# Attention's values move into the ring of five weight buffers, are asked for two groups ahead, and q and k get a sixth buffer

## The chip, the core and the metric

The kernel runs on one core of a Trainium2 chip. The core has five engines that run their own instruction streams in order and meet at semaphores: TensorE (PE, matrix products; its weight loads are shown as PEld), VectorE (DVE), ScalarE (ACT), GpSimd (POOL) and SyncE (SP, which here does nothing but issue transfers). Transfers between HBM and on-chip memory run on 16 DMA engines. The metric is device time in microseconds (us) of one execution, the median of the runs.

## What is computed

Three steps in a row: attention with a sigmoid instead of a softmax, a mixture of 8 experts in which every token gets exactly one expert, and a two-layer network with a squared ReLU.

```python
batch, n_heads, seq, head_dim = (4, 12, 448, 64)
scores = scale * np.matmul(q, k.transpose(0, 1, 3, 2)) - np.log(S)
attn = 1.0 / (1.0 + np.exp(-scores))
x = np.matmul(attn, v)                      # then laid out as 1792 tokens x 768
logits = x @ w_gate                         # 1792 x 8; greedy assignment, 224 tokens per expert
h = np.maximum(x[mask] @ w1[e], 0.0); out[mask] = h @ w2[e]
r = np.maximum(x @ w_in, 0.0); y = (s * (r * r) + b) @ w_out
```

The change lies in the first step alone.

## The kernel before

**Groups.** The 12 heads of 4 batches make 24 pairs of heads, and two pairs make a group: 12 groups (`NQ`), three to a batch. The loop `for q in range(NQ)` runs over the groups, and each pass has two halves.

**What one group costs each engine.** `scores(q + 1, ...)` makes the products of keys and queries of the next group on PE, in seven units of 128 (or, for unit 3, 2 x 64) keys; after each, ACT takes the sigmoid into a tile `attn`. Outside the first group a score is the sum of three products of rounded halves, `wh` and `wl`, which DVE makes from the raw q and k of a pair in `split_qk(n)` (two instructions). The small unit 3 takes the raw tile itself. `values(q, half)` then multiplies `attn` by the values: 12 PE instructions on blocks of 128 keys (line 334 in the first kernel) and, at the start of the second half, 8 on the last 64 keys of the two pairs (line 328). So 448 keys of two pairs are 2 x 3 blocks of 128 and one block that holds 64 of each pair.

**Other work in the loop.** DVE also converts the last network's weights in 24 pieces of 128 x 768 (`convert`, lines 152 to 169), each read as 768 KB (`cv_in`, tile `craw`, three buffers) and written back as 384 KB (`cv_out`, `nw<-co`). At the first group of batches 1 to 3 the gate of the batch before is worked out (`gate`, `gate_turn`, `prefs`), and in the last three groups four tiles of the first expert's weights are fetched and split (`w_dma` line 235, `w_high` line 244 on ACT, `w_low` line 254 on DVE).

**Order of the transfers.** Almost every transfer is issued by SP, in the order of the code, and SP stands still at each until what it overwrites is free: `cv_in` waits until DVE has read the `craw` tile (line 155), `cv_out` until the converted piece is done. Besides, each transfer waits until the one eight places before it has landed, since eight semaphores go round. In pass q SP is given q and k of pairs 2q + 5 and 2q + 6 (`load_qk`, lines 273 and 274, 224 KB each), then the values of group q + 1 (`load_v`, line 268, 448 KB), and behind them the pieces of the two conversions.

**Buffers.** Tile `rqk` holds q and k of one pair: five buffers. Tile `vt` holds the values of one group, 7 blocks of 128 x 128: two buffers. The ring `wraw`, five buffers of 6 blocks of 128 x 128 (384 KB), holds raw weights from the end of attention on and lies unused until then.

After the loop come the assignment of tokens to experts (the auction) and, with three quarters of the time, the experts and the last network, in which PE is fed from `wraw`.

Of the kernel before, what the change touches and what calls it, by code (L numbers as in the profile page):

```python
# [8 lines left out]
F32 = mybir.dt.float32  # L9
# [10 lines left out]
B, H, S, D = 4, 12, 448, 64  # L20
# [26 lines left out]
NQ = B * NP // 2  # L47
# [15 lines left out]


@with_exitstack
def tile_kernel(ctx, tc, qT, kT, v, wg, w1, w2, wi, wo, s2, b2, cst, out):
    nc = tc.nc
    V, A, G, T = nc.vector, nc.scalar, nc.gpsimd, nc.tensor

    const = ctx.enter_context(tc.tile_pool(name="const", bufs=1))  # L70
    wraw = ctx.enter_context(tc.tile_pool(name="wraw", bufs=5))
# [48 lines left out]
    cgp = early.enter_context(tc.tile_pool(name="cgp", bufs=1))  # L120

    att = ExitStack()
    qk = att.enter_context(tc.tile_pool(name="qk", bufs=5))
    vp = att.enter_context(tc.tile_pool(name="vp", bufs=2))
    at = att.enter_context(tc.tile_pool(name="at", bufs=2))
    ps_s = att.enter_context(tc.tile_pool(name="ps_s", bufs=3, space=PSUM))
# [9 lines left out]
    def cv_in():  # L136
        if todo:
            i = todo.pop(0)
            src, k, n = wide[i]
            craw[i] = cgp.tile([128, 768, 2], I32, name="craw", bufs=3)  # L140
            nc.sync.dma_start(craw[i].rearrange("p a b -> p (a b)"), src[n].bitcast(I32).rearrange("p k c -> p (k c)"))
            coming.append(i)
# [117 lines left out]
        nu["use"] += 1  # L260
        return splits.pop(i)

    raw_qk, two_qk, vt, attn, pvs, plg, lgs, pts = {}, {}, {}, {}, {}, {}, {}, {}
    pairs = [(b, p) for b in range(B) for p in range(NP)]

    def load_v(q):
        vt[q] = vp.tile([128, 7, 128], F32, name="vt", bufs=2)
        nc.sync.dma_start(vt[q], v[q // 3, q % 3])

    def load_qk(i):  # L270
        b, p = pairs[i]
        r = qk.tile([128, 2, S], F32, name="rqk")
        nc.sync.dma_start(r[:, 1], kT[b, p])
        nc.sync.dma_start(r[:, 0], qT[b, p])
        raw_qk[i] = r

    def split_qk(i):
        r = raw_qk[i]
        h = wsp.tile([128, 2 * S], F32R, name="wh")
        lo = wlp.tile([128, 2 * S], F32R, name="wl")  # L280
        r = r.rearrange("p a s -> p (a s)")
        V.tensor_copy(h, r)
        V.tensor_sub(lo, r, h.bitcast(F32))
        two_qk[i] = [a.rearrange("p (a s) -> p a s", a=2) for a in (h, lo)]
# [4 lines left out]
    def scores(q, units):  # L289
        if q >= NQ:  # L290
            return
        for r in units:
            p = ps_s.tile([128, 2, 512], F32, name="psc")
            if r == 3:
                work = [(2 * q + n, slice(HD, S), slice(n * 64, n * 64 + 64)) for n in range(2)]
            else:
                c = r % 4
                work = [(2 * q + r // 4, slice(c * 128, (c + 1) * 128), slice(0, 128))]
            plain = q < PLAIN or r == 3
            n_terms = 1 if plain else 3  # L300
            for m in range(n_terms):
                for j in range(2):
                    me = slice(j * D, (j + 1) * D)
                    for n, keys, rows in work:
                        if plain:
                            kx = qx = raw_qk[n]
                        else:
                            h, lo = two_qk[n]
                            kx, qx = ((h, h), (lo, h), (h, lo))[m]
                        T.matmul(p[rows, j, :S], kx[me, 1, keys], qx[me, 0], start=(m == 0),  # L310
                                 stop=(m == n_terms - 1), skip_group_check=True)
            attn[q, r] = at.tile([128, 2, S], F32, name="attn", bufs=8)
            A.activation(attn[q, r], p[:, :, :S], AF.Sigmoid, bias=nls, scale=1.0 / math.sqrt(D))  # L313
        if units[-1] == 6:
            for n in (2 * q, 2 * q + 1):
                raw_qk.pop(n)
                if q >= PLAIN:
                    two_qk.pop(n)

    def values(q, block):  # L320
        v = vt[q]
        pvs[q, block] = pv = ps_v.tile([128, 512], F32, name="pv")
        if block:
            a = attn.pop((q, 3))
            for n in range(2):
                rows = slice(n * 64, n * 64 + 64)
                for j in range(2):
                    T.matmul(pvs[q, n][j * 64:(j + 1) * 64, :S], v[rows, 3, j * D:(j + 1) * D], a[rows, j],
                             start=(n == 1), stop=(n == 0), skip_group_check=True)
            done(q, 0)  # L330
        for c in range(3):
            a = attn.pop((q, 4 * block + c))
            for j in range(2):
                T.matmul(pv[j * 64:(j + 1) * 64, :S], v[:, 4 * block + c, j * D:(j + 1) * D], a[:, j],  # L334
                         start=(block == 0 and c == 0), stop=(block == 1 and c == 2), skip_group_check=True)
        if block:
            done(q, 1)

    def done(q, n):
        b, p = pairs[2 * q + n]  # L340
        pv = pvs.pop((q, n))
        xt = xT[:, p, b * S:(b + 1) * S]
        if (q, n) == (NQ - 1, 1):
            A.copy(xt[:, :2 * CP], pv[:, :2 * CP])
            A.copy(xt[:, 2 * CP:], pv[:, 2 * CP:S])
        else:
            A.copy(xt, pv[:, :S])
# [9 lines left out]
    def gate_copy(b):  # L357
        lgs[b] = at.tile([128, S], F32, name="lg", bufs=1)
        A.copy(lgs[b], plg.pop(b)[:, :S])
# [65 lines left out]
    load_qk(1)  # L425
    nc.sync.dma_start(ct, cst)
    load_v(0)
    G.memset(wgs, 0.0)
    nc.sync.dma_start(wgs[:, :, :E], wg)
    load_qk(2)  # L430
    load_qk(3)
    cv_in()
    cv_in()
    cv_in()
    scores(0, range(7))
    load_qk(4)
    nc.sync.dma_start(sb2[:, 0:1], s2.partition_broadcast(128))
    nc.sync.dma_start(sb2[:, 1:2], b2.partition_broadcast(128))
    G.memset(on, 1.0)
# [12 lines left out]
    for q in range(NQ):  # L452
        b, t = divmod(q, 3)
        closing = b == B - 1
        for n in (2 * q + 5, 2 * q + 6):
            if n < 2 * NQ:
                load_qk(n)
        if q + 1 < NQ:
            load_v(q + 1)
        for half in range(2):  # L460
            if q + 2 < NQ:
                split_qk(2 * q + 4 + half)
            values(q, half)
            if t == 0 and b:
                if half:
                    gate_turn(b - 1, True)
                    prefs(b - 1)
                else:
                    gate(b - 1, 0, NP, NP)
                    gate_copy(b - 1)  # L470
            if closing and 1 <= 2 * t + half <= 4 and 2 * t + half != 2:
                bracket((2 * t + half) // 2)
            if closing and t == 2 and not half:
                gate(b, 0, NP - 2, NP - 2)
                gate_copy(b)
            scores(q + 1, range(4, 7) if half else range(4))
            n = 2 * (NQ - q) - half
            if 2 < n <= 6:
                w_dma()
            for _ in range({4: 1, 3: 1, 2: 2}.get(n, 0)):  # L480
                w_high()
            for _ in range(CONV[2 * q + half]):
                convert()
            while nu["low"] < nu["high"]:
                w_low()
# [800 lines left out]
def _layout(np, i):  # L1286
    c = np.ascontiguousarray

    def heads(a):
        return a.reshape(B, NP, 2, S, D)  # L1290

    vv = i["v"].reshape(B, 3, 2, 2, S, D)
    main = (vv[..., :HD, :].reshape(B, 3, 2, 2, 3, 128, D).transpose(0, 1, 2, 5, 4, 3, 6)
            .reshape(B, 3, 2, 128, 3, 128))
    tail = vv[..., HD:, :].transpose(0, 1, 2, 4, 3, 5).reshape(B, 3, 128, 1, 128)

    return {
        "qT": c(heads(i["q"]).transpose(0, 1, 2, 4, 3).reshape(B, NP, 128, S)),
        "kT": c(heads(i["k"]).transpose(0, 1, 2, 4, 3).reshape(B, NP, 128, S)),
        "v": c(np.concatenate([main[:, :, 0], tail, main[:, :, 1]], axis=3)),  # L1300
        "wg": c(i["moe_w_gate"].reshape(KD, 128, E).transpose(1, 0, 2)),
        "w1": c(i["moe_w1"].reshape(E, KD, 128, KF, 128).transpose(0, 3, 2, 1, 4)),
        "w2": c(i["moe_w2"].reshape(E, KF, 128, KD, 128).transpose(0, 3, 1, 2, 4).reshape(E, KF, KD, 128, 128)
                .transpose(0, 1, 3, 2, 4)),
        "wi": c(i["moe2_w_in"].reshape(KD, 128, KG, 128).transpose(2, 1, 0, 3)).view(np.int64),
        "wo": c(i["moe2_w_out"].reshape(8, 2, 128, 2, DH).transpose(3, 0, 2, 1, 4)
                .reshape(KG, 128, KD, 128)).view(np.int64),
        "s2": c(i["moe2_s"]),
        "b2": c(i["moe2_b"]),
        "cst": _consts(np),  # L1310
    }
# [17 lines left out]
```

## Time and profile before

| | before |
|---|---|
| median of 3 runs | 881.94 us (879.71 to 887.55) |
| profiled execution, time | 882.63 us |
| profiled execution, span of the core | 880.8 us |
| PE busy | 856.3 us, 97% of the span |
| PEld / DVE / ACT / POOL busy | 746.9 / 642.6 / 509.4 / 85.0 us |
| mean granted TensorE clock | 0.987 |
| attention | from the start to about 158 us |

Times in the trace are microseconds from the start of the span. Attention is the part in which PE's rows carry `psc` (scores, gate) and `pv` (values). In a timeline or chain row the first number is the start, the second the length; an "x12" merges twelve instructions of one line, and square brackets give the idle time ahead of the row and what ended it. The granted clock is given as a share of full speed: 1.00 is 2.4 GHz and 0.50 is 1.2 GHz.

### The profile page before, as it was taken

To read this page: it belongs to the slowest core of one execution; us is meant where nothing else is said; L and a number is where in the kernel's file an instruction comes from. 1 tells how busy PE (TensorE), PEld (TensorE's weight loads), DVE (VectorE), ACT (ScalarE), POOL (GpSimd) and SP (SyncE) were. 2 spreads that over 40 slices of the span, in tenths; PEclk is the share of its full clock that TensorE was granted. 3 is DMA by queue.
4 is the path that set the end of the run, shared out by engine and by line. 5 is a ranking of instruction groups with operands and counts; after the bars stand their busy time and mean duration, and the time that the engine had idled before them with its cause. 6 is when DMAs were issued, how large, how long until landed. Compare 5 with 4: busy or idle time off the path is not lost.

```text
span 880.8 us, 14238 instructions
## 1 busy us (share of the span) xinstructions
PE 856.3 (97%) x5188; PEld 746.9 (85%) x5188; DVE 642.6 (73%) x1113; ACT 509.4 (58%) x887; POOL 85.0 (10%) x146
## 2 busy tenths in 40 slices
PE   9898999879999999999999999999999999999997
PEld 4444454649999999999999999999999999999997
DVE  2978786756778776779768776877887766857681
ACT  6466567745755566753565546767666555645440
POOL 1000000123000000000155422000000000000003
PEclk9899999999999999999999999999999999999999
DMA  8889796666668786658899987676653433332313
GB/s 297 303 295 353 268 381 231 187 205 223 208 200 287 244 291 208 209 187 304 280 335 319 301 238 247 194 234 185 225 180 98 128 107 116 112 106 91 101 37 132
DMA packets 76778, 190.40 MB, mean 216 GB/s; under 512 B 9120, under 2 KB 31136, under 8 KB 76448
## 3 DMA queue, kind: packets, MB, share of 16 engines
q1 hardware_dynamic: 68800, 164.28, 55.7%
q0 software_dynamic: 7904, 25.17, 10.1%
q8 instruction: 42, 0.69, 0.3%
q14 instruction: 32, 0.26, 0.1%
HBM read 161.11 MB, written 42.47 MB: 231 GB/s over the span
## 4 chain that ended last, share of the span: by engine, by line
PE 89%; DMA 5%; DVE 2%; ACT 1%; issue 1%; SPq 1%; POOL 0%; POOLq 0%; DVEq 0%; ACTq 0%
PE acc L757 16%; PE acc L758 8%; PE acc L1072 7%; PE acc L1071 7%; PE acc L1069 7%; PE pv L334 6%; PE psc L310 5%; PE acc L915 4%; PE acc L914 4%; PE acc L916 4%; PE acc L1178 4%; PE acc L1180 4%; PE acc L1179 4%; DMA vt<-in_v_dram 3%; PE acc L783 1%; PE acc L784 1%
## 5 line engine op out<-in xcount | busy, mean ns | idle before, releaser
L244 ACT CAST wh<-raw 128x768 fp32r<-128x768 f32 (+1 forms) x248 | 201.5, 823 | 91.0 <-issue 66.5
L254 DVE TENSOR_TENSOR wl<-raw,wh 128x768 fp32r<-128x768 f32 (+1 forms) x248 | 229.5, 937 | 21.3 <-PE acc L1071 11.3
L757 PE MATMUL acc<-u,wh 128*128 128x448 f32 x384 | 120.8, 374 | 0.0
L758 PE MATMUL acc<-u,wl 128*128 128x224 f32 x384 | 101.6, 265 | 0.2 <-DVE wl L254 0.2
L757 PE MATMUL acc<-x,wh 128*128 128x448 f32 x288 | 95.0, 384 | 0.6 <-issue 0.6
L313 ACT ACTIVATE attn<-psc,nls 128x896 f32<-128x896 f32 x84 | 78.0, 1009 | 29.9 <-PE psc L310 29.9
L758 PE MATMUL acc<-x,wl 128*128 128x224 f32 x288 | 76.9, 267 | 0.0
L757 PEld LDWEIGHTS acc<-u,wh 128*128 128x128 f32 x384 | 72.0, 188 | 5.3
L758 PEld LDWEIGHTS acc<-u,wl 128*128 128x128 f32 x384 | 73.3, 191 | 0.4 <-DVE wl L254 0.4
L334 PE MATMUL pv<-attn,vt 128*64 128x448 f32 x288 | 62.9, 574 | 8.5 <-DMA vt<-in_v_dram 8.5
L914 PE MATMUL acc<-y,wh 128*128 128x448 f32 x192 | 70.8, 369 | 0.0
L915 PE MATMUL acc<-y,wh 128*128 128x448 f32 x192 | 70.2, 366 | 0.0
L916 PE MATMUL acc<-y,wl 128*128 128x448 f32 x192 | 70.1, 365 | 0.0
L762 ACT COPY tmp<-acc 128x224 f32<-128x224 f32 x96 | 33.0, 343 | 48.9 <-PE acc L758 48.6
L757 PEld LDWEIGHTS acc<-x,wh 128*128 128x128 f32 x288 | 55.0, 191 | 4.8 <-issue 0.9
L334 PEld LDWEIGHTS pv<-attn,vt 128*64 128x64 f32 x288 | 19.7, 141 | 44.5 <-issue 41.6
L1069 PE MATMUL acc<-wh,as 128*128 128x384 f32 x168 | 56.1, 334 | 0.0
L1071 PE MATMUL acc<-wl,as 128*128 128x384 f32 x168 | 56.1, 334 | 0.0
L1072 PE MATMUL acc<-wh,as 128*128 128x384 f32 x168 | 56.1, 334 | 0.0
L758 PEld LDWEIGHTS acc<-x,wl 128*128 128x128 f32 x288 | 55.8, 194 | 0.3 <-DVE wl L254 0.3
L763 DVE TENSOR_TENSOR tmp<-acc,tmp 128x224 f32<-128x224 f32 x78 | 30.1, 385 | 27.9 <-ACT tmp L762 27.5
L648 POOL DMA_INDIRECT xr<-xs,idx x16 | 16.8, 1050 | 262.2 <-PE px L748 250.1
(338 smaller groups left out, 1974.2 us busy)
## 6 DMA issues: line engine op xcount, KB each, us to landing
raw<-in_w_dram SPq DMA_DIRECT2D x128, 384.0 KB, 3.8
raw<-nw SPq DMA_DIRECT2D x64, 384.0 KB, 3.7
craw<-in_wi_dram SPq DMA_DIRECT2D x16, 768.0 KB, 6.6
raw<-mx SPq DMA_DIRECT2D x32, 384.0 KB, 5.0
nw<-co SPq DMA_DIRECT2D x24, 384.0 KB, 7.3
craw<-in_wo_dram SPq DMA_DIRECT2D x8, 768.0 KB, 6.1
ra<-in_wo_dram SPq DMA_DIRECT2D x8, 768.0 KB, 5.3
hs<-nw POOLq DMA_DIRECT2D x16, 384.0 KB, 9.7
```

Source lines behind the costliest of these rows:

```text
L244: A.copy(h, r)
L254: eng.tensor_sub(lo, r, h.bitcast(F32))
L313: A.activation(attn[q, r], p[:, :, :S], AF.Sigmoid, bias=nls, scale=1.0 / math.sqrt(D))
L334: T.matmul(pv[j * 64:(j + 1) * 64, :S], v[:, 4 * block + c, j * D:(j + 1) * D], a[:, j], start=(block == 0 and c == 0), stop=(block == 1 a ...
L757: T.matmul(p[:, :2 * CAP], wh, src[:, k].rearrange("p a s -> p (a s)"), start=(k == 0), stop=False)
L758: T.matmul(p[:, :CAP], wl, src[:, k, 0], start=False, stop=(k == n - 1))
L914: T.matmul(p, wh, src[:, k, 0], start=first, stop=False)
L915: T.matmul(p, wh, src[:, k, 1], start=False, stop=False)
L916: T.matmul(p, wl, src[:, k, 0], start=False, stop=last)
L1069: T.matmul(acc, hi, wh[:, cols], start=(opens[j] and u == 0 and c == 0), stop=False, skip_group_check=True)
L1071: T.matmul(acc, hi, wl[:, cols], start=False, stop=False, skip_group_check=True)
L1072: T.matmul(acc, lo, wh[:, cols], start=False, stop=(u == 3 and c == 1), skip_group_check=True)
```

## The change

Four things, all in attention:

1. The values of a group are a tile of the ring `wraw` (six blocks, 384 KB, name `raw`), and `vt`'s two buffers are gone.
2. The blocks that hold the last 64 keys are taken out of `v` into an input of their own, `vrest`: one tile `vr` of three blocks (192 KB, two buffers) for the three groups of a batch, loaded with the batch's first group.
3. `load_v` runs two groups ahead: in pass q it asks for group q + 2, and group 1 is asked for before the loop, between the first and the second `cv_in`.
4. `rqk` has six buffers, and `load_qk` runs one pair further ahead: pairs 4 and 5 are asked for before the first scores, and pass q asks for 2q + 6 and 2q + 7.

```diff
 def load_v(q):
-    vt[q] = vp.tile([128, 7, 128], F32, name="vt", bufs=2)
+    vt[q] = wraw.tile([128, 6, 128], F32, name="raw")
     nc.sync.dma_start(vt[q], v[q // 3, q % 3])
+    if q % 3 == 0:
+        vr[q // 3] = vp.tile([128, 3, 128], F32, name="vr")
+        nc.sync.dma_start(vr[q // 3], vrest[q // 3])

-    qk = att.enter_context(tc.tile_pool(name="qk", bufs=5))
+    qk = att.enter_context(tc.tile_pool(name="qk", bufs=6))

 def values(q, block):
-    v = vt[q]
+    v, rest = vt[q], vr[q // 3][:, q % 3]
...
-                T.matmul(..., v[rows, 3, j * D:(j + 1) * D], a[rows, j], ...)
+                T.matmul(..., rest[rows, j * D:(j + 1) * D], a[rows, j], ...)
...
-            T.matmul(..., v[:, 4 * block + c, j * D:(j + 1) * D], a[:, j], ...)
+            T.matmul(..., v[:, 3 * block + c, j * D:(j + 1) * D], a[:, j], ...)

 load_qk(2)
 load_qk(3)
 cv_in()
+load_v(1)
 cv_in()
 cv_in()
+load_qk(4)
+load_qk(5)
 scores(0, range(7))
-load_qk(4)

 for q in range(NQ):
-    for n in (2 * q + 5, 2 * q + 6):
+    for n in (2 * q + 6, 2 * q + 7):
         if n < 2 * NQ:
             load_qk(n)
-    if q + 1 < NQ:
-        load_v(q + 1)
+    if q + 2 < NQ:
+        load_v(q + 2)
```

The instructions of PE, DVE, ACT and POOL stay the same and in the same order; SP has four transfers more (the four `vr`) and another order. Line numbers behind line 268 grow by three to five: 310 becomes 313, 334 becomes 337.

The start of SP's queue before, from the first conversion tile on. `craw` is a conversion tile, `rqk` q or k of a pair (here pairs 4, 5 and 6), `sb` two constants, `vt` the values of group 1; in brackets what the transfer waits for (DMAHW is the transfer eight places before it):

```order
L141 DMA craw<-in_wi_dram 128x1536 [waits DMAHW3_49]
L141 DMA craw<-in_wi_dram 128x1536 [waits DMAHW4_49]
L141 DMA craw<-in_wi_dram 128x1536 [waits DMAHW5_49]
L273 DMA rqk<-in_kT_dram 128x448 [waits DMAHW6_49]
L274 DMA rqk<-in_qT_dram 128x448 [waits DMAHW7_49]
L437 DMA sb_76<-in_s_dram 128x1 [waits DMAHW0_49]
L438 DMA sb_76<-in_b_dram 128x1 [waits DMAHW1_49]
L273 DMA rqk<-in_kT_dram 128x448 [waits DMAHW2_49,PE_49]
L274 DMA rqk<-in_qT_dram 128x448 [waits DMAHW3_49]
L273 DMA rqk<-in_kT_dram 128x448 [waits DMAHW4_49,PE_49]
L274 DMA rqk<-in_qT_dram 128x448 [waits DMAHW5_49]
L268 DMA vt<-in_v_dram 128x896 [waits DMAHW6_49]
```

The same place of the changed kernel, up to the constants; the `raw` tile is the values of group 1, and the two pairs are 4 and 5:

```order
L141 DMA craw<-in_wi_dram 128x1536 [waits DMAHW4_49]
L268 DMA raw<-in_v_dram 128x768 [waits DMAHW5_49]
L141 DMA craw<-in_wi_dram 128x1536 [waits DMAHW6_49]
L141 DMA craw<-in_wi_dram 128x1536 [waits DMAHW7_49]
L276 DMA rqk<-in_kT_dram 128x448 [waits DMAHW0_49]
L277 DMA rqk<-in_qT_dram 128x448 [waits DMAHW1_49]
L276 DMA rqk<-in_kT_dram 128x448 [waits DMAHW2_49]
L277 DMA rqk<-in_qT_dram 128x448 [waits DMAHW3_49]
L442 DMA sb_76<-in_s_dram 128x1 [waits DMAHW4_49]
L443 DMA sb_76<-in_b_dram 128x1 [waits DMAHW5_49]
```

Group 1's values moved from behind pair 6 to ahead of the second conversion tile, and pairs 4 and 5 stand behind them, 384 KB later than before; ahead of this place one `vr` tile was added.

The other end of attention, SP's queue in passes 10 and 11 before: the last group's values, the third and fourth tile of expert weights and the last converted pieces:

```order
L268 DMA vt<-in_v_dram 128x896 [waits DMAHW5_49,PE_49]
L235 DMA raw<-in_w_dram 128x768 [waits DMAHW6_49]
L147 DMA nw_156<-co 128x768 [waits DMAHW7_49,DVE_49]
L235 DMA raw<-in_w_dram 128x768 [waits DMAHW0_49]
L147 DMA nw_157<-co 128x768 [waits DMAHW1_49,DVE_49]
```

And in the changed kernel, where the last values were already asked for in pass 9:

```order
L235 DMA raw<-in_w_dram 128x768 [waits DMAHW2_49,PE_49]
L147 DMA nw_156<-co 128x768 [waits DMAHW3_49,DVE_49]
L235 DMA raw<-in_w_dram 128x768 [waits DMAHW4_49,DVE_49]
L147 DMA nw_157<-co 128x768 [waits DMAHW5_49]
```

The two weight tiles now wait for a reader of the values that lay in their buffer: the third for PE, the fourth for a DVE instruction behind PE's last reading of group 10's values.

## Rows read from the trace of the kernel before

**Rows 1.** The page's costliest groups, PE's products with the values; last, idle ahead.

```profile
L334 PE MATMUL pv<-attn,vt 128*64 128x448 f32 x288 | 62.9, 574 | 8.5 <-DMA vt<-in_v_dram 8.5
```

**Rows 2.** Timeline of PE: start, us, engine, line, operation, [idle before <-releaser].

```profile
13.58 0.47 PE L310 MATMUL psc<-wh,wl 64*128 64x448 f32 x2 [0.39 <-DVE wl L283]
...
26.26 4.75 PE L334 MATMUL pv<-attn,vt 128*64 128x448 f32 x12 [4.64 <-DMA vt<-in_v_dram]
...
63.64 2.48 PE L334 MATMUL pv<-attn,vt 128*64 128x448 f32 x12
...
74.28 2.48 PE L334 MATMUL pv<-attn,vt 128*64 128x448 f32 x12
...
88.29 3.67 PE L334 MATMUL pv<-attn,vt 128*64 128x448 f32 x12 [3.31 <-DMA vt<-in_v_dram]
```

**Rows 3.** The chain that ended last, in order of time: start, us, what.

```profile
19.19 6.93 DMA vt<-in_v_dram
...
31.01 3.25 PE psc L310 x25
...
52.94 1.63 PE psc L354 x12
54.57 3.05 PE psc L310 x26
...
80.95 7.20 DMA vt<-in_v_dram
...
91.96 2.08 PE psc L354 x12
```

**Rows 4.** Windows: stretch, length, busy of five engines, granted clock, DMA share, GB/s.

```profile
16.00:20.00 4.00, 4.00 (x31) 1.48 (x24) 0.17 (x1) 2.78 (x5) 0.00 (x0) 1.00 0.69 250
...
26.30:31.00 4.70, 4.70 (x14) 1.37 (x14) 4.53 (x8) 0.00 (x0) 0.00 (x0) 0.50 0.67 242
31.00:50.00 19.00, 19.00 (x141) 10.53 (x140) 15.70 (x23) 13.18 (x17) 0.00 (x0) 0.99 0.95 342
...
36.00:40.00 4.00, 4.00 (x30) 2.24 (x28) 3.93 (x6) 2.45 (x4) 0.00 (x0) 1.00 1.02 417
...
50.00:84.90 34.90, 34.52 (x250) 18.10 (x248) 30.23 (x45) 23.12 (x30) 0.00 (x0) 1.00 0.89 312
...
88.30:94.00 5.70, 5.70 (x26) 1.68 (x26) 5.53 (x8) 0.00 (x0) 0.00 (x0) 0.70 0.97 344
```

**Rows 5.** Timeline of SP's queue: issue of single transfers.

```profile
13.01 0.33 SPq L273 DMA_DIRECT2D rqk<-in_kT_dram  x1
14.83 0.33 SPq L274 DMA_DIRECT2D rqk<-in_qT_dram  x1
16.76 0.33 SPq L273 DMA_DIRECT2D rqk<-in_kT_dram  x1
18.65 0.33 SPq L274 DMA_DIRECT2D rqk<-in_qT_dram  x1
...
141.11 0.42 SPq L235 DMA_DIRECT2D raw<-in_w_dram  x1
```

**Rows 6.** What SP's queue waited for: total us, times, longest.

```profile
SPq L141 <- DVE co L155: 66.4, 20, 9.3
```

**Rows 7.** Timeline of DVE: first halves of pairs 2, 4 and 6; a later reduction.

```profile
11.77 0.63 DVE L282 CAST wh<-rqk 128x896 fp32r<-128x896 f32 x1 [2.10 <-DMA rqk<-in_qT_dram]
...
19.83 0.63 DVE L282 CAST wh<-rqk 128x896 fp32r<-128x896 f32 x1 [4.64 <-DMA rqk<-in_qT_dram]
20.49 1.09 DVE L283 TENSOR_TENSOR wl<-rqk,wh 128x896 fp32r<-128x896 f32 x1
...
29.95 0.62 DVE L282 CAST wh<-rqk 128x896 fp32r<-128x896 f32 x1
...
146.94 0.26 DVE L397 TENSOR_REDUCE m<-mt 2x1 f32<-2x112 f32 x1 [0.64 <-ACT mt L396]
```

**Rows 8.** Landing of q and k, of expert weights; ACT's last two casts in attention.

```profile
DMA to landing us min/median/max: 2.5/5.9/9.3
...
raw<-in_w_dram SPq DMA_DIRECT2D x128, 384.0 KB, 3.8
...
152.50 1.57 ACT L244 CAST wh<-raw 128x768 fp32r<-128x768 f32 x2
```

## What is predicted, and from which rows

> **What bounds the kernel now.** I read the page's costliest groups first. PE is busy for nearly the whole span, so only two things can shorten it: idle time ahead of a PE row, or PE rows that run slower than their like. Among the large PE groups one has idle time that a transfer ended: the products with the values, 8.5 us, all put down to the values' transfer [rows 1]. PE's timeline shows where: 4.64 us at 26.26, 3.31 us at 88.29, and the rest (0.55) in two waits of under 0.4 [rows 2].
>
> Next I looked at the rows behind each wait. Twelve products with the values take 2.48 us where PE has been running (63.64, 74.28), but 4.75 us behind the first wait and 3.67 behind the other [rows 2]. The windows say why: the granted clock is 0.50 from 26.3 to 31.0, that is 1.2 GHz, and 0.70 as a mean over 88.3 to 94, against 0.99 in 31 to 50 [rows 4]. So each of the two long waits is paid twice: as idle time and as slow rows behind it.
>
> Then why the values are late. In the chain of waits, group 1's transfer is issued at 19.19 and takes 6.93, group 6's at 80.95 and takes 7.20 [rows 3]. Both left SP late. At the start SP goes transfer by transfer: the issues at 13.01, 14.83, 16.76 and 18.65 [rows 5] each wait for the transfer eight places earlier, and group 1's values stand behind all of them. Later SP waits behind DVE: 66.4 us in all until a conversion tile has been read [rows 6], and the loads of a pass stand behind that wait. Since the values are asked for one group ahead (a group takes PE 74.28 - 63.64 = 10.64 us, rows 2), any slip of SP by three or four us makes PE wait.
>
> **What the change removes.** (a) The waits. Group 1's values are now issued ahead of five large transfers. I reckon landings in order, as the start shows them: the issues in [rows 5] mark the landing, eight places back, of pair 3's q (13.01), and of the three conversion tiles (14.83, 16.76, 18.65): 768 KB in about 1.9 us, 404 KB per us. Pair 3's q would land at 13.4 (0.35 later, see below), the first conversion tile 1.8 later at 15.2, and group 1's 384 KB 0.95 us behind it: 16.1. PE wants them at 21.6, when its scores are done (26.26 - 4.64). That is 5 us to spare. Later groups are asked for 10.64 us earlier than before against a worst lateness of 3.31. Nothing is left of the waits: -8.5.
>
> (b) The slow rows behind them. Values 4.75 - 2.48 = 2.27 and 3.67 - 2.48 = 1.19 [rows 2]; scores 3.25 - 3.05 = 0.20 and gate 2.08 - 1.63 = 0.45 [rows 3]. Together 4.1. The clock stayed at 0.99 to 1.00 from 31 to 84.9, where PE hardly paused [rows 4], so I take all of it: -4.1. If the clock fell anyway this term would be nothing, which is the upper bound of this part.
>
> (c) DVE's waits for q and k, such as 2.10 and 4.64 [rows 7], shrink with the sixth buffer. They are off PE's path today, so I count them as nothing by themselves; they matter for what PE can wait for next.
>
> **What it adds.** (d) Four transfers of 192 KB; each group's values shrink by 64 KB, so the bytes are the same overall. Only the first sits ahead of something urgent. Before pair 2's q and k lie now 128 KB more; at 404 KB per us that is 0.32, say 0.35 us. DVE's split of pair 2 starts the moment they land (11.77, rows 7), and PE waits for its second half (0.39 at 13.58, rows 2), so this goes straight on the path: +0.35. Below it could be 0, if the smaller tile of group 0 lets PE start as much earlier; above, if the extra transfer cost as much as a lone one, the shortest landing of q or k, 2.5 [rows 8].
>
> The Trainium skill, "DMA: Bandwidth & Descriptors", section on the anatomy of one DMA, puts a fixed cost of about 2.0 us on a transfer besides its bytes (fitted for transfers that GpSimd issues); by it the tile would cost 2.4 us as an estimate and the sum would be some 2 us smaller. The trace speaks against adding it up: conversion tiles land 1.9 us apart with all their bytes [rows 5]. No run here shows the 192 KB transfer yet.
>
> (e) Pairs 4 and 5 stand behind group 1's values and the conversion tiles. Pair 4 matters: PE's scores of group 2 need its halves. By the same reckoning the second and third conversion tile land at 18.0 and 19.9, pair 4 at 21.1 (224 KB each for k and q, 0.6 us), against 19.83 today [rows 7]. Its split is over 1.75 us later (19.83 to 21.58, rows 7), at 22.9. PE is through group 1's first values at 21.6 + 0.35 + 2.4 = 24.4. It has 1.5 us to spare: cost 0. If the transfers ran at 250 GB/s, the window at 16 to 20 [rows 4], that is 244 KB per us, the 1984 KB behind 16.1 would land at 24.2, the split end at 26.0, and PE wait 1.6. I take 0, since [rows 5] are from the same stretch and full transfers ran at 404; 1.6 is kept for the range.
>
> (f) From there DVE must keep up, as PE comes some 7 us earlier while DVE does not. Two halves of a pass take DVE 29.95 - 19.83 = 10.1 us [rows 7] and PE 10.64: the spare time grows by half a us per group. At group 4 DVE has a second conversion (about 3 us more), but before it PE has a gate more than DVE (1.63, rows 3). So the spare time does not fall below 1.5. Cost 0.
>
> (g) The ring. Values take turns with weights: the fourth weight tile lies in group 10's buffer. It was issued at 141.11 [rows 5]; now it must wait for a DVE instruction behind PE's last reading, at the latest the reduction at 146.94 [rows 7], so 147.2 on today's clock. It lands 3.8 later [rows 8], at 151.0. ACT casts the third and fourth tile at 152.50 to 154.07 [rows 8], the fourth from 153.3. 2.3 us to spare: cost 0. Without that cover ACT would hold back the copy of the last group, and PE with it, at most by a landing of 9.3 [rows 8]: 156.5 - 153.3 = 3.2. Behind it in SP stands a write that nobody waits for.
>
> **The sum.** -8.5 - 4.1 + 0.35 = -12.25. The profiled execution took 882.63 with a span of 880.8; it would be 870.4. The median of the runs is 0.7 below it, so the median should be 881.94 - 12.25 = 869.7.
>
> **The rivals.** *The wait changes its name.* PE no longer waits for values but for the split of pair 4, or for pair 2. For it: pair 4 lands later than today, and 1.5 us is little. Against it: the landings in order at 404 KB per us. Price: up to 1.6 of (e) or up to 2.15 more of (d) (2.5 against 0.35), rarely both: 871.3 to 873.
>
> *The DMA engines become the bound.* A group moves 2 x 768 + 2 x 384 + 4 x 224 + 448 = 3648 KB, 3.74 MB; at PE's 10.64 us that is 351 GB/s. For it: the share was already 0.95 at 342 GB/s in 31 to 50, and 0.89 at 312 in 50 to 84.9 [rows 4]; both make about 350 to 360 at a full share. Against it: in these same stretches PE ran at its full pace with this load, and 36 to 40 shows 417 [rows 4]. At 330 GB/s a group takes 11.3, 0.7 more; over eight groups 5.5, less the 1.5 to spare: 4. That gives 873.7.
>
> *The ring holds the weights back* (g): 3.2 at most, 872.9.
>
> *Slower than before.* The mechanism is again the transfers' rate, as conversions and loads now run without the pauses in which they caught up. The gain of 12.25 over 11 groups is 1.1 us each: when a group takes 11.75 us, which is 318 GB/s, all is eaten. At 300 GB/s a group takes 12.5, 1.8 x 11 = 20 us lost, and the time is 890. The mean of 312 in 50 to 84.9 speaks for it only if the 0.89 share beside it were the most that can be had; 417 in 36 to 40 says that it is not.
>
> *It does nothing.* The values would have to come as late as today. Their issue two groups ahead stands in the order of the queue, and 5 us to spare is a lot; only a slip of SP by over 14 us in a later group would do it, and SP's longest wait is 9.3 [rows 6]. 880 to 882.
>
> **How the numbers follow.** Forecast, 867 to 871: 0.6. The wait with another name, 871 to 873: 0.2. DMA bound without a loss, 872 to 878: 0.1. The ring, 870 to 873: 0.04. Nothing: 0.02. Slower: 0.04. The likeliest gives 869.7. The range goes down by the spread of the runs shown (the lowest of before is 2.2 below its median) and the whole of (d), to 866.5, and up through the renamed wait and half the DMA case to 875.5; about 0.85 lies inside. About 1%, 8.8 us, is what a measurement of this kernel can tell from no change. Under 873.1 lie the forecast, the renamed wait, most of the ring and some of the DMA case, less a little for what I overlooked: 0.8. Within 1%: 0.16. Slower: 0.04.
>
> **What will show it.** In the changed kernel's page the products with the values should have no idle time that a transfer ended, and 12 of them always take 2.48 us. The clock from 22 to 94 should be near 1.00. PE should begin group 1's values at about 22.0, its scores of group 2 at 24.4 and the rows behind the loop about 12 us before today's. (d) is wrong if the wait at 13.58 grows by more than 0.4; (e) if PE waits for `wl` ahead of group 2's scores; (f) if it does so later; (g) if ACT's casts at the end of attention wait for `raw`. The forecast as a whole fails if PE keeps its full pace but the part behind attention, which has the same instructions, takes longer, or if the waits come back on another tile.

## The result and the profile after

The changed kernel takes 871.13 us (median of 6 runs, 869.78 to 873.94), the kernel before beside it 882.49 (6 runs, 879.71 to 887.55). The ratio is 0.9868, with a 95% interval of 0.9838 to 0.9898. That is 1.3% faster, 11.4 us at the medians. The forecast was 869.7 with a range of 866.5 to 875.5 and a chance of 0.8 for faster by over 1%.

The profiled execution took 870.04 us, with a span of 868.2 (before 882.63 and 880.8). From its page, the row of the products with the values that answers to [rows 1], and the clock in 40 slices:

```profile
L337 PE MATMUL pv<-attn,raw 128*64 128x448 f32 x288 | 59.4, 548 | 0.0
...
PEclk9999999989999999999999999999999999999999
```

The idle time of 8.5 us that a transfer ended is gone, and the same 288 products take 3.5 us less. The values now lie in a tile named `raw`. PE's timeline at the places of [rows 2] (start, us, engine, line, operation, in brackets the idle time before):

```profile
4.35 7.28 PE L313 MATMUL psc<-rqk 64*128 64x448 f32 x32
11.56 2.48 PE L337 MATMUL pv<-attn,raw 128*64 128x448 f32 x12
...
14.47 0.47 PE L313 MATMUL psc<-wh,wl 64*128 64x448 f32 x2
...
22.47 2.48 PE L337 MATMUL pv<-attn,raw 128*64 128x448 f32 x12
24.88 0.47 PE L313 MATMUL psc<-wh 64*128 64x448 f32 x2
...
78.14 2.48 PE L337 MATMUL pv<-attn,raw 128*64 128x448 f32 x12
```

PE begins group 1's values at 22.47 without a wait, where it waited until 26.26, and twelve products take 2.48 everywhere. The windows that answer to [rows 4] (stretch, length, busy of PE, PEld, DVE, ACT, POOL, granted clock, DMA share, GB/s):

```profile
22.00:94.00 72.00, 72.00 (x516) 37.33 (x514) 69.74 (x101) 48.42 (x61) 0.00 (x0) 1.00 0.95 351
22.00:147.00 125.00, 124.72 (x899) 65.27 (x896) 112.85 (x171) 83.93 (x110) 0.00 (x0) 1.00 0.88 323
60.00:84.00 24.00, 24.00 (x178) 12.56 (x174) 23.27 (x35) 16.30 (x20) 0.00 (x0) 1.00 0.98 358
```

PE is busy in all of 22 to 94 at a clock of 1.00; before, the same 72 us had 64.06 us of work at a mean clock of 0.93. What DVE and SP waited for in the first 150 us (total us, times, longest):

```profile
DVE wh L285 <- DMA rqk<-in_qT_dram: 8.4, 2, 5.7
...
SPq L141 <- DVE co L155: 38.8, 17, 7.4
```

DVE's waits for q and k fell from 15.8 us in eight places to 8.4 in two, both at the start, and SP's waits behind DVE from 66.4 [rows 6] to 38.8. DVE's timeline at the last two gates of attention, in the changed kernel and then in the one before:

```profile
124.05 0.43 DVE L383 TENSOR_TENSOR ge<-L 112x256 f32<-112x256 f32 x1 [3.20 <-ACT L L379]
146.30 0.43 DVE L383 TENSOR_TENSOR ge<-L 112x256 f32<-112x256 f32 x1 [0.39 <-ACT L L379]
```

```profile
158.03 0.43 DVE L380 TENSOR_TENSOR ge<-L 112x256 f32<-112x256 f32 x1 [0.35 <-ACT L L376]
```

So 11.73 us of the 12.6 by which the span shrank are won by the end of attention.

### The profile page after: what moved, and what is told of

The parts are those of the page before. It is cut to its first block, busy times and chain, and to the rows that moved or that the text cites. A ratio compares the mean times of both kernels' runs of the same rounds, so it can differ in the third digit from the quotient of the medians.

```text
span 868.2 us, 14236 instructions
## 1 busy us (share of the span) xinstructions
PE 853.3 (98%) x5188; PEld 744.6 (86%) x5188; DVE 642.7 (74%) x1113; ACT 508.7 (59%) x887; POOL 85.7 (10%) x146
## 4 chain that ended last, share of the span: by engine, by line
PE 93%; DVE 2%; ACT 1%; DMA 1%; issue 1%; POOL 0%; POOLq 0%; ACTq 0%; DVEq 0%
PE acc L762 15%; PE acc L763 7%; PE psc L313 7%; PE pv L337 7%; PE acc L1076 7%; PE acc L1074 7%; PE acc L1077 7%; PE acc L919 4%; PE acc L920 4%; PE acc L921 4%; PE acc L1183 4%; PE acc L1185 4%; PE acc L1184 4%; PE acc L788 1%; PE acc L789 1%; PE acc L790 1%
## 5 line engine op out<-in xcount | busy, mean ns | idle before, releaser
L337 PE MATMUL pv<-attn,raw 128*64 128x448 f32 x288 | 59.4, 548 | 0.0
L337 PEld LDWEIGHTS pv<-attn,raw 128*64 128x64 f32 x288 | 18.5, 136 | 34.8 <-issue 32.0
```

Of the source, the lines that this page charges most:

```text
L337: T.matmul(pv[j * 64:(j + 1) * 64, :S], v[:, 3 * block + c, j * D:(j + 1) * D], a[:, j], start=(block == 0 and c == 0), stop=(block == 1 a ...
```

## The experiments

Three things are to be told apart: which part of the change brings the gain (values earlier, the sixth q and k buffer, the place where the values lie), whether the slow rows hang on the waits, and whether the longer start or the DMA engines limit what is left. "Before" below is the median of the runs of the kernel before on the same chip: 881.19 (28 runs) for the first four, 881.12 (7) for the next four, 881.99 (11) for the last four.

### Group 1's values early, the rest as before

```diff
 cv_in()
+load_v(1)
 cv_in()
...
-        if q + 1 < NQ:
+        if q and q + 1 < NQ:
```

> The kernel before with one edit: group 1's values are asked for ahead of the second conversion tile; later groups still one group ahead, two buffers of seven blocks, five q and k buffers. Theory A (the values are late because SP's queue is paced by DVE, so only asking two groups ahead cures it): the wait of 4.64 us goes, PE comes about 7 us earlier to groups 2 and 3, but their values are issued when they were (30.8 and 42.0), so PE waits there for about 5 to 7 us in all and again at group 6; the time stays within 2 us of before, 880 to 882. Theory B (each wait stands for itself): 4.64 + 2.27 + 0.20 = 7.1 us go for good and the wait of 3.31 at group 6 stays as it is, 875.

Median 883.2, ratio 1.0029 (1.0004 to 1.0053). PE's waits for values, on its timeline and in the sum over the first 150 us:

```profile
39.32 4.05 PE L334 MATMUL pv<-attn,vt 128*64 128x448 f32 x12 [6.64 <-DMA vt<-in_v_dram]
...
88.11 2.48 PE L334 MATMUL pv<-attn,vt 128*64 128x448 f32 x12 [2.08 <-DMA vt<-in_v_dram]
```

```profile
PE pv L334 <- DMA vt<-in_v_dram: 8.7, 2, 6.6
```

The wait at 26.26 is gone and stands at the next group, longer: 8.7 us in all against 8.5. Group 2's values were issued at 32.26, behind a conversion tile that waits for DVE, and took 6.92. One load moved ahead gives nothing, since PE comes earlier to the next load, which SP issues no earlier. The slow rows go with the long wait too: behind 6.64 us the twelve products take 4.05, behind 2.08 they take 2.48.

### Only the sixth q and k buffer

```diff
-    qk = att.enter_context(tc.tile_pool(name="qk", bufs=5))
+    qk = att.enter_context(tc.tile_pool(name="qk", bufs=6))
...
+    load_qk(5)
     scores(0, range(7))
...
-        for n in (2 * q + 5, 2 * q + 6):
+        for n in (2 * q + 6, 2 * q + 7):
```

> The kernel before with the other half alone: six q and k buffers, loads of q and k one pair further ahead; values as before. Theory A (q and k off the path, but SP paced by DVE): DVE's waits for q and k fall from 15.8 to about 8 us, the ones at the start staying; group 1's values stand behind one pair more, so the first wait grows by about 1.1 us to 5.7; from 48 us on DVE and SP run about 2.8 us earlier, so the wait at group 6 shrinks from 3.31 to under 1 and its slow rows (1.64) go: 877 to 880. Theory B (it does nothing): 882. Theory C (the sixth buffer carries the gain): about 871.

Median 881.77, ratio 1.0015 (0.9988 to 1.0043): no difference. Waits, and DVE's timeline at one gate:

```profile
PE pv L334 <- DMA vt<-in_v_dram: 8.5, 4, 3.9
DVE wh L282 <- DMA rqk<-in_qT_dram: 7.0, 2, 4.7
```

```profile
100.43 0.43 DVE L380 TENSOR_TENSOR ge<-L 112x256 f32<-112x256 f32 x1 [7.52 <-ACT L L376]
```

DVE's waits for q and k shrink to 7.0, but PE waits 8.5 us for values as before, and DVE now waits for PE at the gates. That group 6's values would come in time was expected by one theory and did not happen: issued at 79.37 instead of 80.95, they still cost 3.25. Nor did the first wait grow to 5.7, as that theory had it: it was 3.88.

### Only the values earlier, with five q and k buffers, twice

The changed kernel with the lines of the sixth buffer taken back:

```diff
-    qk = att.enter_context(tc.tile_pool(name="qk", bufs=6))
+    qk = att.enter_context(tc.tile_pool(name="qk", bufs=5))
...
-    load_qk(4)
-    load_qk(5)
     scores(0, range(7))
+    load_qk(4)
...
-        for n in (2 * q + 6, 2 * q + 7):
+        for n in (2 * q + 5, 2 * q + 6):
```

> The changed kernel with q and k as before: five buffers, loaded as before; values in the ring, two groups ahead, with the tile of rests. Theory A (the gain is the values' alone and DVE has just enough to spare): no wait for values, PE waits for split halves 0 to 2 us in all, 871 to 873. Theory B (the sixth buffer is needed, as PE is now 12 us earlier and DVE still waits for q and k at 48, 85 and 95): DVE's waits of 2.8, 2.3 and 1.4 come through to PE, 874 to 878.

> The run with the values alone once more, on the same chip as the two with their own buffers. Its seven times lay in two clumps, 871.4 to 872.3 and 874.5 to 876.4. Theory A (the wait for the fourth weight tile is there in some executions and not in others): again 871 to 876, median 872 to 875, and above the run with five q and k buffers and own pool by 1 to 3. Theory B (chance between chips): equal to it within 1.

Medians 874.53 (871.41 to 876.4) and 871.8 (870.33 to 877.49), ratios 0.9905 (0.9877 to 0.9934) and 0.9901 (0.9870 to 0.9932). No wait for values is left in either, so the values alone bring most of the gain. What remains shows on ACT's and PE's timelines of the first:

```profile
144.46 0.83 ACT L244 CAST wh<-raw 128x768 fp32r<-128x768 f32 x1 [3.19 <-DMA raw<-in_w_dram]
```

```profile
145.78 1.74 PE L375 MATMUL psc<-wgs,xT 128*112 128x8 f32 x16 [1.64 <-ACT xT L350]
```

The fourth weight tile was issued at 137.11 (changed kernel 134.57), ACT waited for it, and PE for ACT. The tile went out 2.5 us later and took 7.3 to land (137.11 to 144.46). DVE, which waited 17.7 us for q and k here, came to the second-last gate at 129.21 and found its data there, where in the changed kernel it stands ready at 120.85 and waits 3.20 for PE. The second profile has 14.8 us of such waits, DVE at 127.23, the tile issued at 135.14, and no wait of ACT: so some executions lose there and others don't.

### The waits filled with products of zeros

In the kernel before, useless products of zeros (the helper that it has for its start) stand ahead of the two late groups of values:

```diff
+            if half == 0 and q in (1, 6):
+                keep_clock(18 if q == 1 else 13, small_psum()[:CP])
```

> The kernel before plus idle products of zeros on PE ahead of the values of group 1 (18) and group 6 (13), about 3.9 and 2.8 us at 0.216 us each, inside the waits of 4.64 and 3.31; nothing else changes. It parts the two prices of a wait. Theory A (the slow rows behind a wait come of PE's standing still): the waits stay as long, the rows behind them take 2.48 instead of 4.75 and 3.67, and 2.27 + 0.20 + 1.19 + 0.45 = 4.1 us go: 878. Theory B (the rows are slow because their data or PSUM is late, not the clock): 882. If the values come later because PE is earlier elsewhere, the waits would grow: the waits' rows tell.

PE's timeline, and the windows behind the filled places:

```profile
21.42 4.07 PE L418 MATMUL psc<-zero 128*112 128x512 bf16 x18
26.36 2.48 PE L334 MATMUL pv<-attn,vt 128*64 128x448 f32 x12 [0.87 <-DMA vt<-in_v_dram]
...
49.32 2.48 PE L334 MATMUL pv<-attn,vt 128*64 128x448 f32 x12 [1.22 <-DMA vt<-in_v_dram]
...
83.75 3.01 PE L418 MATMUL psc<-zero 128*112 128x512 bf16 x13
86.69 2.48 PE L334 MATMUL pv<-attn,vt 128*64 128x448 f32 x12
```

```profile
22.00:31.00 9.00, 8.13 (x51) 4.39 (x53) 8.78 (x13) 2.42 (x4) 0.00 (x0) 1.00 0.66 225
84.00:94.00 10.00, 10.00 (x68) 5.03 (x69) 8.26 (x11) 4.32 (x6) 0.00 (x0) 1.00 0.97 350
```

Group 1's values begin at 26.36, as late as before (26.26), but take 2.48 instead of 4.75, and the clock stays at 1.00, where it was 0.50 from 26.3 to 31 and 0.70 from 88.3 to 94 [rows 4]. So the slow rows do come from PE's standing still: the data came as late as before, and only what PE did ahead of it had changed. The time won was partly spent again: new waits of 0.29 and 1.22 at groups 2 and 3, since PE now comes earlier to values that don't. The profile's attention ended 3.2 us sooner, at 154.81; the median, 880.65, ratio 0.9989 (0.9962 to 1.0016), can't be told from no change.

### The small tile and the constants moved back at the start

First only the first `vr` tile behind pair 3:

```diff
     load_qk(3)
+    load_rest(0)
     cv_in()
```

> The changed kernel with one transfer moved: the first batch's rests (192 KB) are asked for behind pair 3's q and k, not ahead of pair 2's. In the changed kernel DVE's split of pair 2 begins at 12.66 against 11.77 before. Theory A (the extra transfer ahead of pair 2 costs its issue and its bytes): the split begins at 11.7 to 12.0 again, the rests still land before PE wants them at about 16, and up to 0.9 us go, all of it seen in the rows and little in the times: 870 to 871. Theory B (the later start is the clock's or chance): the split stays at 12.5 or later.

Then also the table of constants behind them, with DVE's copies of it behind the splits of pair 2:

```diff
-    nc.sync.dma_start(ct, cst)
...
     load_qk(3)
+    load_rest(0)
+    nc.sync.dma_start(ct, cst)
...
+    split_qk(2)
+    split_qk(3)
```

> The same, and besides the table of constants (634 KB), whose first reader that matters comes much later, is asked for behind pair 3 and the rests, with DVE's copies of it behind the splits of pairs 2 and 3. Theory A (at the start PE waits for nothing but bytes ahead of what it needs): at 404 KB per us pair 2 lands 1.6 us earlier than in the run with the late rests, DVE's split begins at about 10.3, PE is then held only by the sigmoids of group 0, and 1 to 1.5 us go: 868.5 to 870. Theory B (the start is bound by ACT's seven sigmoids, which end at 11.7 at the earliest): under 0.5 us.

Medians 871.79 and 870.97, ratios 0.9874 (0.9839 to 0.9910) and 0.9881 (0.9848 to 0.9913): both as the changed kernel. In the first, the split of pair 2 begins at 12.21, between what the two theories gave (11.7 to 12.0, or 12.5 and later), so it decides nothing. In the second, DVE and PE:

```profile
9.07 0.63 DVE L289 CAST wh<-rqk 128x896 fp32r<-128x896 f32 x1 [7.92 <-DMA rqk<-in_qT_dram]
```

```profile
4.35 6.30 PE L317 MATMUL psc<-rqk 64*128 64x448 f32 x32
10.58 2.48 PE L341 MATMUL pv<-attn,raw 128*64 128x448 f32 x12
```

The split of pair 2 begins at 9.07 instead of 12.66, 3.6 us earlier, yet PE's first values begin only 1.0 earlier (10.58 against 11.56), because they wait for the first scores and their activations, not for pair 2. Behind them PE is 1.3 us ahead of the first profile of the changed kernel (group 0's second values begin at 16.72 against 18.01), and stays so to the end of attention (145.01 against 146.30). How much of it is pair 2's is not shown: the first scores were shorter here too, by 1.0 us, for a reason that differs from execution to execution (see the last section).

### More to load

The changed kernel with a load of 384 KB that nobody reads in each of passes 0 to 8:

```diff
+        if q < 9:
+            spare = vp.tile([128, 6, 128], F32, name="spare", bufs=1)
+            nc.sync.dma_start(spare, v[q // 3, q % 3])
```

> The changed kernel with a useless load of 384 KB more in each of passes 0 to 8, behind the values in SP's queue (10% more bytes in attention). It measures how far the DMA engines are from being the bound. Theory A (they are not): 0 to 1.5 us more, no wait of PE above 1 us, 871 to 873. Theory B (they are, at about 350 GB/s): a group takes 4032 KB, 4.13 MB, that is 11.8 us instead of 10.64, 1.1 us more in each of nine groups less the 1.3 us to spare: 880.

Median 870.38, ratio 0.9866 (0.9836 to 0.9896). The windows:

```profile
22.00:147.00 125.00, 124.72 (x899) 65.54 (x898) 112.58 (x171) 83.46 (x109) 0.00 (x0) 1.00 0.93 349
60.00:84.00 24.00, 24.00 (x178) 12.31 (x176) 22.00 (x32) 16.52 (x21) 0.00 (x0) 1.00 1.01 367
```

26 GB/s more over the whole of attention (349 against 323) cost PE nothing: 124.72 us of products in 125 as without it. DVE waited 3.7 us for a conversion's write, which it could spare. The DMA engines are near full here and still not what limits the kernel.

### The values in buffers of their own

To see whether the shared ring delays the weights, the values got a pool of three buffers of their own, with five and with six q and k buffers:

```diff
-        vt[q] = wraw.tile([128, 6, 128], F32, name="raw")
+        vt[q] = vp.tile([128, 6, 128], F32, name="vt", bufs=3)
```

> The kernel of the run with the values alone (five q and k buffers, values two groups ahead), but the values lie in three buffers of their own, so the weight tiles at the end of attention wait for no values. In that run the fourth weight tile was issued at 137.11, when DVE had finished the first tile's low half (136.13 to 137.08), ACT stood 3.19 us for it and PE 1.64 behind. Theory A (the ring is what the five q and k buffers are short of: DVE is late, the fourth tile waits for DVE, ACT waits for the tile): no wait of ACT for a weight tile at the end, attention ends 1.5 to 2 us earlier, 871 to 872.5. Theory B (DVE's waits for q and k cost in themselves): 874 to 875 again.

> The changed kernel with the values in three buffers of their own instead of the ring, everything else as changed. Theory A (where the values lie is of no matter as long as DVE is in time): within 1 us of the changed kernel, 870 to 872. Theory B (the ring holds the weights back in the changed kernel too): 869 or less, and ACT's last casts of attention earlier.

With five: median 872.96, ratio 0.9904 (0.9879 to 0.9930). With six: 871.51, ratio 0.9882 (0.9853 to 0.9911). ACT's timeline with five, and SP's queue ahead of it:

```profile
144.10 0.83 ACT L244 CAST wh<-raw 128x768 fp32r<-128x768 f32 x1 [1.34 <-DMA raw<-in_w_dram]
145.94 0.83 ACT L244 CAST wh<-raw 128x768 fp32r<-128x768 f32 x1 [1.01 <-DMA raw<-in_w_dram]
```

```profile
135.72 0.33 SPq L141 DMA_DIRECT2D craw<-in_wo_dram  x1
136.09 0.42 SPq L235 DMA_DIRECT2D raw<-in_w_dram  x1
137.09 1.03 SPq L235 DMA_DIRECT2D raw<-in_w_dram  x1
```

My theory of the ring fell here: with free buffers the weight tiles still come late. The rows point to DVE, which is late itself (20.6 us of waits for q and k): the third tile stands in SP's queue behind a conversion tile that waits for DVE, and the two then took 8.0 and 8.8 us to land. That attention would end earlier than in the run with the values alone did not come either: it ended at 150.18, against 147.77 there.

With five buffers this profile shows a second price of late q and k, which the sum of PE's waits leaves out. The products of unit 3 read the raw tiles of q and k, and twice they stood until one had landed, as DVE did for the same tile:

```profile
108.35 0.63 DVE L285 CAST wh<-rqk 128x896 fp32r<-128x896 f32 x1 [1.68 <-DMA rqk<-in_qT_dram]
...
108.79 0.58 PE L313 MATMUL psc<-rqk 64*64 64x448 f32 x3
```

The last of the eight products began 1.46 us after the first here (from 107.37) and 1.41 at 84.36, against 0.55 in the changed kernel: 1.8 us lost in the middle of attention, where the other profiles with early values lose nothing. So the other theory, that DVE's waits for q and k cost in themselves, holds at least for this execution (874.75). The repeated run with the values alone (871.8) was expected 1 to 3 us above the kernel with own buffers and five; it came out 1.2 below, with intervals that overlap.

With six buffers the place of the values makes no difference. Their sharing of the weights' buffers saves memory, not time.

### The changed kernel twice more

> The changed kernel once more, for a second profile. In its first profile the first scores take 7.28 us against 5.89 before, as PE's rows at 4.35 to 7.4 are spaced like slow ones. Theory A (the clock's state at the start is chance from run to run): the first scores take 5.9 to 7.3 and the split of pair 2 still begins at about 12.6. Theory B (the changed order of loads slows the start): 7.2 to 7.4 again.

> The changed kernel on the same chip, as the measure for the three others: 870 to 872. Attention ends (DVE's last ranking of the gate) within 1 us of 146.3, the first profile's; first scores take 5.9 to 7.3 us, chance at the start.

Medians 871.25 and 871.19, ratios 0.9883 (0.9852 to 0.9914) and 0.9881 (0.9853 to 0.9910). Their profiles show the same steps with some scatter at the start (split of pair 2 at 11.40 and 13.10) and end attention at 145.43 and 146.62. Seven sets of runs with early values and six buffers (three of them of the changed kernel itself) lie between 0.9866 and 0.9883, the three with five buffers between 0.9901 and 0.9905: about 2 us, though the interval of each alone overlaps the others'. Taken together, the 30 runs with six buffers have a mean of 871.2 and the 19 with five one of 873.5.

## Why the prediction was right, step by step

**The waits (a).** -8.5 as reckoned. SP's issue that waits for group 1's values, eight places behind them:

```profile
16.61 0.33 SPq L443 DMA_DIRECT2D sb<-in_b_dram  x1
```

So they had landed by 16.61 (forecast 16.1), and PE took them at 22.47 (forecast 22.0). What carries the gain is that all groups are asked for two ahead: one early load alone moved the wait to its neighbour. That is the rival of the renamed wait, seen in that experiment and, as a wait for raw q and k, in one with five buffers, not in the changed kernel.

**The slow rows (b).** -4.1 as reckoned: the products with the values alone take 3.5 us less on the page. Filling the waits confirmed the cause in the rows; in the median it could not be told from no change.

**The sixth buffer (c).** "Nothing by themselves" held for the buffer alone. That it matters for "what PE can wait for next" was right too, but I had not seen where: at the end of attention, where an early DVE lets SP ask for the last weight tiles in time, and in one profile with five buffers at the raw tiles of two pairs. By the ratios it is worth about 2 us, lost in some executions and not in others.

**The small tile (d).** This term is the one that the runs do not settle. The forecast was +0.35, straight on the path through the split of pair 2. In the four profiles without the tile (before and the experiments built on it) the split begins at 11.62 to 12.18, mean 11.87; in eight with it (all built on the changed kernel except the two that moved it back) at 11.40 to 13.10, mean 12.50: +0.6, with ranges that overlap. In the first profile the row after it came 0.89 later (14.47 against 13.58). But PE waited there for nothing: its first scores, the same 32 products, took 7.28 instead of 5.89. So the path ran over the first scores, which the sum had left out, and not over the tile's landing. In three other profiles with the tile PE did wait for the split, 0.30 to 0.86 us, where it waited 0.39 before. And the longer first scores need not be the tile's doing: with the tile moved back they took 7.22.

The Trainium skill, "DMA: Bandwidth & Descriptors", section on the anatomy of one DMA, gives a fixed cost of about 2.0 us besides the bytes, fitted for transfers that GpSimd issues; by it the tile would have cost 2.4 as an estimate. The trace does not bear that out: the means of this case stand 0.6 apart, and with the tile moved back the split began at 12.21, 0.3 before the mean. The measurement decides: no such cost shows in a queue with other transfers around the tile.

**Pair 4 (e).** DVE's timeline, the first halves of pairs 2 and 4:

```profile
12.66 0.63 DVE L285 CAST wh<-rqk 128x896 fp32r<-128x896 f32 x1 [2.64 <-DMA rqk<-in_qT_dram]
...
21.80 0.63 DVE L285 CAST wh<-rqk 128x896 fp32r<-128x896 f32 x1 [5.72 <-DMA rqk<-in_qT_dram]
```

Forecast: pair 4 landed at 21.1, split through at 22.9, PE there at 24.4. Measured: 21.80, 23.55 and 24.88, so 1.3 to spare instead of 1.5.

**DVE's keeping up (f).** PE waited for no half of a pair afterwards.

**The ring (g).** DVE's, SP's and ACT's rows:

```profile
133.58 0.96 DVE L254 TENSOR_TENSOR wl<-raw,wh 128x768 fp32r<-128x768 f32 x1 [2.52 <-ACT wh L244]
```

```profile
134.57 0.33 SPq L235 DMA_DIRECT2D raw<-in_w_dram  x1
```

```profile
140.76 1.57 ACT L244 CAST wh<-raw 128x768 fp32r<-128x768 f32 x2
```

The fourth weight tile went out when DVE had read the first (133.58 + 0.96). On the old clock I allowed it until 147.2, some 135 on the new one. With the median landing of 3.7 it is there at 138.3, 3.2 before ACT's second cast (141.5). In the two other executions of the changed kernel it landed after 3.4 and 3.6, with 3.5 and 3.3 to spare. The reckoning leans on that landing: before, the same tile took 7.2 (141.11 to 148.32), and with five buffers 7.3. The 3.19 that ACT waited with five buffers is the price which I had put on the ring, and the tile did wait for the ring there. But with a pool of its own ACT waited as well, 2.35 in two waits, so the ring is not needed for it; what both profiles share is a late DVE.

**The sum.** With 0.89 instead of 0.35 for the start it is -8.5 - 4.1 + 0.89 = -11.71; the end of attention moved by -11.73. So the two large terms hold in this pair of executions. The small one is luck: measured where group 0's second values begin (17.12 before), the start lost 0.89, 0.02 and 1.33 us in the three executions of the changed kernel, and each kept that, to within 0.2 us, to the end of attention. The forecast for the profiled execution was 870.4; three executions of the changed kernel took 870.04, 871.24 and 870.89. The median forecast was 1.4 too low, and the gain of 11.4 at the medians is 0.9 less than forecast. That lies within what the interval leaves open (0.9838 to 0.9898 of 882.49 is 9.0 to 14.3 us).

**The rivals.** The DMA engines as the bound, and with them the slower outcome, fall by the kernel that loads 384 KB more per pass at no cost. No version ran measurably better than the changed kernel.

## What to carry to other kernels

Where one queue issues loads behind waits on an engine's progress, moving a single late load moves the wait to the next one; ask for the whole stream far enough ahead that no pass depends on the queue's pace. Count a long wait with the slow rows behind it, and take the rows of like work that ran without a wait as the measure (here 2.48 against 4.75; the waits for values of 3.25 us and more had slow rows behind them, those of 2.08 and less had not). A buffer that gives nothing alone can still keep the engine that paces the queue early, so try it with and without the other part of the change.

## What the runs showed of the hardware beyond that

**The first scores.** The same 32 products at 4.35 took 5.89 to 6.41 us in the four profiles with the old loads and 6.11 to 7.80 in ten with the new ones. The views give a granted clock of 1.00 there in all, but they give that also where the trace has no record of the clock, and its record begins only later: at 4.09 in the kernel before and at 7.18 in the first profile of the changed one. PE's weight loads show what lies ahead of it, first in the changed kernel:

```profile
6.75 0.34 PEld L313 LDWEIGHTS psc<-rqk 64*128 64x128 f32 x2 [0.41 <-issue]
7.35 0.19 PEld L313 LDWEIGHTS psc<-rqk 64*128 64x128 f32 x2 [0.26 <-issue]
```

and before, at the start and in the stretch of clock 0.50 behind the first wait:

```profile
4.73 0.19 PEld L310 LDWEIGHTS psc<-rqk 64*128 64x128 f32 x2 [0.18 <-issue]
...
31.10 0.34 PEld L310 LDWEIGHTS psc<-wh,wl 64*128 64x128 f32 x2
```

A pair of loads takes 0.34 where the clock is on record as 0.50 and 0.19 at 1.00. So the first profile of the changed kernel ran its first scores at the lower level, 1.2 GHz, until about 7.2, and the kernel before only until about 4.1, behind the same seven products of zeros from 1.18 on. The moment differs between executions of one kernel: the record begins at 7.18, 6.02 and 5.80 in the three of the changed kernel. The second cause is q of pair 1, which landed at 6.18 before and at 7.60 to 8.59 in five of the ten profiles; in the third of the changed kernel PE's row shows the wait:

```profile
8.72 3.43 PE L313 MATMUL psc<-rqk 64*64 64x448 f32 x18 [0.26 <-DMA rqk<-in_qT_dram]
```

Whether the new loads make either likelier is not shown. The kernel with the small tile moved back asks for its first tiles in the order of the kernel before, and has both (6.29 and 8.01).

**The clock behind attention.** PE's products with the first expert's weights, a row and a window (in the order of [rows 4], PE to POOL) in the first profile of the changed kernel and in its third:

```profile
186.89 0.38 PE L762 MATMUL acc<-x,wh 128*128 128x448 f32 x1
...
186.50:190.10 3.60, 3.58 (x23) 3.45 (x24) 0.67 (x2) 1.44 (x3) 0.49 (x1) 1.00 0.64 189
```

```profile
187.28 0.60 PE L762 MATMUL acc<-x,wh 128*128 128x448 f32 x1
...
186.60:190.10 3.50, 3.50 (x12) 3.24 (x13) 0.36 (x1) 0.00 (x0) 0.62 (x1) 0.50 0.56 175
```

The same kernel runs this stretch at either level. In the first profile the clock was at 0.50 from 174.4 to 181.3, ahead of these products. In the third it rose at 179.9, PE then stood for most of the time, and at 183.3 it fell again, until 190.1. From the first expert's first product to the first one with its second matrix it is 16.55 us in the first profile and 18.0 to 18.9 in the thirteen others, 18.27 before. So 1.7 us of the first profile's span come from here and not from the change; what follows took 1.0 longer than before (665.2 against 664.2). Together with 0.1 between the two that is the 0.9 by which its span shrank more than its attention.

**Full DMA engines beside full PE.** 367 GB/s at a share of 1.01 over 24 us slowed no product, above the 312 at 0.89 from which one rival was reckoned [rows 4].
